# Column tiles for the global values, a contiguous DFT output, the FFN from slot 37 and its evictions later in the step

## The chip, the cores and the metric

The kernel runs on one NeuronCore of a Trainium2 chip. The metric is the device time of one execution in microseconds; lower is better. The five engines are TensorE (PE), VectorE (DVE), ScalarE (ACT), GpSimd (POOL) and SyncE (SP), each with its own in-order queue; here SP issues all DMAs.

## What is computed

Attention over 8 batches, 8 heads, 512 local and 32 global tokens of width 64, then a mixing layer on the concatenated heads:

```python
s_g   = scale * q_g @ k_all.T ;  out_g = softmax(s_g) @ v_all          # 32 global queries see all 544 keys
s_ll  = where(|i - j| <= 32, scale * q_l @ k_l.T, -1e9)                # local queries: a band ...
s_lg  = scale * q_l @ k_g.T ;    out_l = softmax([s_lg, s_ll]) @ [v_g, v_l]   # ... and the 32 global keys
x     = heads concatenated                                             # (8, 544, 512)
u     = x + real(fft(fft(x, axis=1), axis=2))
un    = (u - mean(u)) / sqrt(var(u) + 1e-6)
out   = u + relu(un @ w_ch1) @ w_ch2                                   # 512 -> 2048 -> 512
```

Matrix products are made of fp16 pieces: each operand is split into a high and a low half (hi, lo), and three products (hi hi, hi lo, lo hi) are added up in PSUM. So every operand has a copy on ScalarE for hi and a subtraction on VectorE or GpSimd for lo.

## The kernel before

**Order.** `run` (L831) writes down every step of the whole kernel with a time in *slots*, sorts by time, and issues the steps in that order; each engine's queue gets its own instructions in this order and nothing is reordered later. `add(slot, rank, f)` places a step at slot + rank, `at(time, f)` on the FFN's own scale. `warp` ties the two: up to slot F0 = 38 they are the same; from there 16 + PAUSE = 22 slots of attention pass beside 32 units (two chunks) of FFN; from slot 60 on, two units a slot. A slot has one attention tile `u` (128 queries of one pair of heads; 128 tiles, with a pause of 6 slots after the first 16).

**Weights.** 32 loads of 128x512 64-bit numbers (n = 0 to 15 are the first layer, k = 0; 16 to 31 the second, k = 1), one a slot from slot -8: `w_load` three slots ahead (SP), `w_abs` (ACT), `w_bits` (L184, four VectorE instructions that make fp32 of the bits), then column scales (`w_max`, `w_fold`, `w_scale`) and `w_split` (L251): for the second layer two ScalarE copies and a GpSimd subtraction. Second-layer weight t is handled at slot 8 + t and split f at slot 26 + f//2, with the scales at 23 to 25. Loads alternate between two buffers that lie where batch 0's DFT input comes later (`rw`) and two (`raw`) that share their place with the FFN's transposed input (`uh`).

**Attention.** For pair p (four slots): `scores` (L380) every second slot, with row halves of the array for the two heads; `masked` on VectorE; `exps`, `p_hi` on ScalarE; `p_lo` on GpSimd; `turn`, a DMA transpose; `values` (L428) at rank 0.60 five slots later; `norm` at 0.66 on VectorE. Global queries go once a pair: `g_scores`, `g_max`, `g_exp`, `g_hi`, `g_lo`, `g_turn`, then `g_values` (L487) and `g_norm` (L496). `g_values` multiplies the 64 rows of both heads' global queries with the values of both heads (130 columns), so half of each product belongs to the wrong head and is not used. `values` and `g_values` write one PSUM bank, `bk`; `values` waits for the `norm` and `g_norm` in front of it.

**DFT.** Once a batch (R = slot of its last tile): `d_load`, sums and differences on VectorE (`d_even`, `d_even2`, `d_tail`) and GpSimd (`d_odd`...), halves (`d_hi`, `d_lo`, `d_tail_hi`, `d_tail_lo`), then `d_first` (L659, five calls of eight matmuls with 137 columns), `d_z`, `d_z2`, `d_second`, `d_as`, `d_df`, `d_add`. `d_first` makes even and odd outputs in two passes and writes each to every second column of its PSUM tile; `d_z` and `d_z2` copy the tile out as it lies.

**FFN.** 17 chunks of 256 rows. Before each: `l_stats`, `l_un`, `l_hi`, `l_lo`, `l_turn` (a DMA transpose), `l_root`. A chunk has eight steps fp of two units: `f_first` (L786, 24 matmuls of 256 columns into one of two PSUM buffers `ps1`), `f_hi` (L799, ScalarE) and `f_lo` (L803, VectorE) that evict it as two halves `h`, and `f_second` (L807, 12 matmuls of 512 columns), which comes after the next step's `f_first`. In units of the step they stand at 0.30, 0.54, 0.65 and 3.30. From slot 60 on half of this is the rank within the slot: `f_hi` at 0.27, `f_lo` at 0.325.

Of the kernel before, what the change touches and what calls it, by code (L numbers as in the profile page):

```python
# [8 lines left out]
F32 = mybir.dt.float32  # L9
# [3 lines left out]
I32 = mybir.dt.int32  # L13
# [14 lines left out]
NVB = 2  # L28
NKB = 2
W0 = -8  # L30
F0 = 38
PAUSE = 6
RS0 = 1.829591166069289e-20


# [54 lines left out]
class Kern:  # L90
# [73 lines left out]
        return self.wd[1][i * P:(i + 1) * P, :]  # L164

    def w_load(self, k, i, n):
        if n % 4 < 2:
            if n == 0:
                rw = self.p1.tile([P, 2, 512, 2], I32, name="rw", tag="x4")
                self.rw = [rw[:, j] for j in range(2)]  # L170
            raw = self.rw[n % 2]
        else:
            raw = self.p2.tile([P, 512, 2], I32, name="raw", tag="uh")
        self.nc.sync.dma_start(raw.rearrange("p n t -> p (n t)"), self.w_src(k, i).bitcast(I32))
        self.raw[k, i] = raw
# [311 lines left out]
    def g_values(self, p):  # L487
        nc, s = self.nc, self.st[p]
        pl, vN = s.pop("plg"), s["v"][0]
        s["pvg"] = pv = self.bk[:64, 260:390].rearrange("p (h d) -> p h d", h=2)  # L490
        for c in range(5):
            n = P if c < 4 else 96
            for m, (a, w) in enumerate(((0, 0), (0, 1), (1, 0))):
                nc.tensor.matmul(pv, pl[:n, 5 * a + c], vN[:n, c, w], start=c == 0 and m == 0, stop=c == 4 and m == 2)  # L494

    def g_norm(self, p):  # L496
        nc, s = self.nc, self.st[p]
        b, hp, pv, sc = s["b"], s["hp"], s.pop("pvg"), s["v"][2]
        dn = self.p2.tile([64, 1], F32, name="dng")
        if hp == 0:  # L500
            self.g[b]["x"] = self.p1.tile([64, 4, 2, D], F32, name="xg")
        nc.vector.tensor_scalar(dn, pv[:, 0, 64:65], 1e-9, sc[:64], op0=ALU.add, op1=ALU.mult)
        nc.vector.reciprocal(dn, dn)
        nc.vector.tensor_scalar_mul(self.g[b]["x"][:, hp], pv[:, :, 0:64], dn)  # L504

    def g_own(self, b):
        xg = self.g[b]["x"]
        return [xg[h * SG:(h + 1) * SG, :, h] for h in range(2)]

    def g_out(self, b):  # L510
        for h, x in enumerate(self.g_own(b)):
            self.nc.sync.dma_start(self.xs[b][0:SG].rearrange("t (p h d) -> h t p d", h=2, d=D)[h], x)
# [146 lines left out]
    def d_first(self, b, i):  # L659
        nc, d = self.nc, self.D[b]  # L660
        eh, ht = d["eh"], d["ht"]
        cs, o, d0, m = (*divmod(i, 2), 0, P) if i < 4 else (0, 0, P, 1)
        d["ps"] = ps = self.d_psum(b)[:m, 0:NK]
        base = (0, 258, 514, 770)[2 * cs + o]
        w = 128 + (base == 0)
        n = NK // 2
        for kp in (1, 0):
            c0, po = n - n * kp, ps[:, 1 - kp:NK:2]
            for k, (a, c) in enumerate(((0, 0), (0, 1), (1, 0))):
                e = base + kp * w + d0  # L670
                nc.tensor.matmul(po, eh[:, a, e:e + m], self.c1[:, cs, c, c0:c0 + n], start=k == 0, stop=False)  # L671
            e = (0, 129, 257, 385)[2 * cs + o] + d0
            nc.tensor.matmul(po, ht[:, e:e + m], self.c1t[:, cs, c0:c0 + n], start=False, stop=True)
# [156 lines left out]

    def run(self):  # L831
        self.h = {}
        late = F0 + 16 + PAUSE

        def warp(t):
            if t < F0:
                return t
            return F0 + 32 * (t - F0) / (16 + PAUSE) if t < late else F0 + 32 + 2 * (t - late)

        plan = Plan(warp)  # L840
        add, at = plan.add, plan.at
# [109 lines left out]
        at(F0 + 32 * 7 + 4.5, self.l_load)  # L951
        for c in range(17):
            F = F0 + 16 * c
            L = F - (6 if c > 1 else 5)
            at(L + .42, self.l_stats, c)
            for j in range(2):
                at(L + j + 1.425, self.l_un, c, j)
                at(L + j + 1.76, self.l_hi, c, j)
                at(L + j + 1.79, self.l_lo, c, j)
                at(L + j + 2.03, self.l_turn, c, j)  # L960
# [62 lines left out]
```

## Time and profile before

| | |
|---|---|
| time, median of 3 (lowest, highest) | 1195.37 us (1194.23, 1196.3) |
| the profiled execution's own time | 1197.24 us |
| its span from first to last instruction | 1195.4 us |
| busy: PE, DVE, ACT, POOL | 84%, 64%, 51%, 42% |
| mean granted PE clock | 0.967 |
| the two costliest groups: `f_first` L796, `f_second` L815 | 383.2 and 381.6 us busy |

Busy time is an average over stages. The trace is cut into stages by the plan's slots; in each, the engine that is busy nearly all the time sets the pace, and where none is, a wait does. Matmuls are pipelined, so what one costs is read from the distance between starts and not from its duration. "[3.09 <-DVE xg L504]" in a timeline row says that the engine stood idle for 3.09 us in front of this instruction until VectorE had finished the one of line 504 that writes xg.

### The profile page before, as it was taken

Reading aid. Unit: us, or ns where it says so; the run is one execution under the profiler, and the core shown is the slowest. Engines: PE = TensorE matmul, PEld = TensorE weight load, DVE = VectorE, ACT = ScalarE, POOL = GpSimd, SP = SyncE. Lnnn points to the kernel's source line nnn. Section 1 sums busy time; section 2 is a strip of 40 time slices with the busy share of each in tenths; the row PEclk is TensorE's granted clock in tenths of the full one; section 3 lists DMA queues with packets and bytes.
Section 4 is the critical chain, followed back from the end, with each engine's and each line's share of the span. In section 5 each row is a group of like instructions: output and inputs, shape, how many; then the busy total and the mean of one; then the engine's idle time right before and its main releaser. Section 6 shows DMA issues by size and latency. Waiting matters only on the chain.

```text
span 1195.4 us, 24283 instructions
## 1 busy us (share of the span) xinstructions
PE 1001.7 (84%) x9351; PEld 717.5 (60%) x9351; DVE 763.1 (64%) x2089; ACT 609.1 (51%) x1348; POOL 508.0 (42%) x473
## 2 busy tenths in 40 slices
PE   0244325399798989998999899999999999999996
PEld 0134225276576767776777677767767666666664
DVE  6999974856757674867486748674766546433221
ACT  4767569576575655655566455646544112111110
POOL 2789278655544634463446344634462211100000
PEclk9999997599898999999999899999999999999999
DMA  7579934557555555555565546555455231120000
GB/s 263 154 178 244 268 75 104 127 116 176 115 138 111 144 117 122 116 139 119 120 115 139 119 119 111 144 119 121 80 110 110 60 87 36 38 55 19 27 27 18
DMA packets 249564, 137.55 MB, mean 115 GB/s; under 512 B 200576, under 2 KB 223200, under 8 KB 249448
## 3 DMA queue, kind: packets, MB, share of 16 engines
q1 hardware_dynamic: 249448, 136.01, 49.0%
q8 instruction: 73, 1.20, 0.4%
q14 instruction: 43, 0.35, 0.1%
HBM read 65.10 MB, written 18.35 MB: 70 GB/s over the span
## 4 chain that ended last, share of the span: by engine, by line
PE 60%; DVE 23%; ACT 8%; POOL 3%; DMA 3%; issue 2%; DVEq 0%; SPq 0%; POOLq 0%; ACTq 0%
PE acc L815 24%; PE ps L796 24%; PE S L394 2%; PE psd L671 2%; DVE pe L404 2%; PE psd L695 1%; PE bk L494 1%; ACT pe L413 1%; PE bk L439 1%; DVE ps L191 1%; DVE ps L192 1%; DVE ps L190 1%; DVE wm L193 1%; PE bk L441 1%; DVE h L805 1%
## 5 line engine op out<-in xcount | busy, mean ns | idle before, releaser
L796 PE MATMUL ps<-uh,wh 128*128 128x256 f16 x3264 | 383.2, 275 | 0.3 <-DMA uh<-unh 0.3
L815 PE MATMUL acc<-wh,h 128*128 128x512 f16 x1632 | 381.6, 384 | 0.0
L796 PEld LDWEIGHTS <-wh 128*128 128x128 f16 x3264 | 320.3, 99 | 59.9 <-issue 0.8
L805 DVE SCALAR_TENSOR_TENSOR h<-ps,h 128x512 f16<-128x512 f32 x136 | 93.7, 689 | 296.2 <-ACT h L801 296.1
L815 PEld LDWEIGHTS <-h 128*128 128x128 f16 x1632 | 155.0, 100 | 173.4 <-issue 11.1
L421 POOL TENSOR_TENSOR ph<-pe,ph 128x448 f16<-128x448 f32 x128 | 134.7, 1053 | 281.5 <-ACT ph L417 111.2
L801 ACT ACTIVATE h<-ps 128x512 f16<-128x512 f32 x136 | 80.3, 591 | 255.8 <-PE ps L796 255.7
L413 ACT ACTIVATE pe<-pe,nm 128x224 f32<-128x224 f32 x256 | 102.0, 469 | 82.3 <-DVE nm L404 82.3
L439 PE MATMUL bk<-vN,pl 128*128 128x65 f16 x768 | 74.5, 205 | 66.7 <-DVE xg L504 34.2
L404 DVE CUSTOM_DVE_ANT_0 pe<-S,msk,z 128x224 f32<-128x224 f32 x256 | 99.6, 445 | 2.9 <-PE S L394 2.9
L441 PEld LDWEIGHTS <-pl 96*128 96x128 f16 x768 | 61.6, 106 | 55.7 <-issue 54.4
L394 PE MATMUL S<-kT,qT 64*128 64x192 f16 x768 | 56.4, 273 | 28.6 <-ACT pg L475 28.3
L439 PEld LDWEIGHTS <-pl 128*128 128x128 f16 x768 | 64.4, 106 | 21.6 <-DMA pl<-ph 15.1
L394 PEld LDWEIGHTS <-qT 64*128 64x128 f16 x1536 | 54.7, 102 | 33.6 <-issue 29.4
L417 ACT ACTIVATE ph<-pe 128x448 f16<-128x448 f32 x128 | 72.0, 562 | 0.0
L372 POOL TENSOR_TENSOR kT<-qk,kT 128x512 f16<-128x512 f32 x32 | 42.7, 1333 | 51.0 <-ACT kT L367 49.8
L762 ACT ACTIVATE unh<-un 128x512 f16<-128x512 f32 x34 | 21.3, 625 | 70.4 <-DVE un L757 70.4
L441 PE MATMUL bk<-vB,pl 96*128 96x65 f16 x576 | 55.7, 205 | 0.0
L357 ACT ACTIVATE qk<-qk,z 128x512 f32<-128x512 f32 x64 | 45.5, 710 | 17.1 <-DVE z L322 17.1
L347 POOL TENSOR_TENSOR vN<-vf,vN 128x640 f16<-128x640 f32 x32 | 46.2, 1443 | 0.3 <-ACT vN L343 0.3
L588 POOL TENSOR_TENSOR s<-x 128x1020 f32<-128x1020 f32 x8 | 18.8, 2348 | 62.0 <-DMA x<-xs 56.3
L372 POOL TENSOR_TENSOR qT<-qk,qT 128x512 f16<-128x512 f32 x32 | 38.7, 1209 | 10.3 <-ACT qT L367 8.6
(182 smaller groups left out, 1638.6 us busy)
## 6 DMA issues: line engine op xcount, KB each, us to landing
qk<-in_qk SPq DMA_DIRECT2D x32, 512.0 KB
vf<-in_v SPq DMA_DIRECT2D x32, 320.0 KB
rw<-in_moe_w_ch SPq DMA_DIRECT2D x16, 512.0 KB
raw<-in_moe_w_ch SPq DMA_DIRECT2D x16, 512.0 KB
xs<-x SPq DMA_DIRECT2D x32, 256.0 KB
out<-u SPq DMA_DIRECT2D x16, 512.0 KB
x<-xs SPq DMA_DIRECT2D x24, 256.0 KB
u<-xs SPq DMA_DIRECT2D x24, 256.0 KB
```

Of the source, the lines that this page charges most:

```text
L372: self.nc.gpsimd.tensor_sub(lo, s.pop(nm), hi)
L394: nc.tensor.matmul(ps, qT[r, a, j], k, start=m == 0, stop=m == 2)
L404: nc.vector.tensor_tensor_reduce(self.per[(4 * p + j) % 4][:, h, 0:224], S[:, h, 224 * n:224 * n + 224], self.msk[:, j], z[:, 8:9], 3e38, ...
L413: nc.scalar.activation(pe[:, h, 0:224], pe[:, h, 0:224], AF.Exp, bias=nm[:, n, h:h + 1], scale=-1.0)
L417: self.nc.scalar.activation(ph[:, 0, :, 0:224], self.per[i % 4][:, :, 0:224], AF.Copy)
L421: self.nc.gpsimd.tensor_sub(ph[:, 1, :, 0:224], self.per[i % 4][:, :, 0:224], ph[:, 0, :, 0:224])
L439: nc.tensor.matmul(pv[:, j % 2, h], pl[:, 4 * a + 2 * h], vN[:, j, c, h, :], start=m == 0, stop=False)
L441: nc.tensor.matmul(pv[:, j % 2, h], pl[0:96, 4 * a + 2 * h + 1], vb, start=False, stop=m == 2)
L796: nc.tensor.matmul(ps[:, q], wt[:, w, c0:c0 + P], uh[:, :, 4 * a + kt, :], start=n == 0, stop=n == 11)
L801: self.nc.scalar.activation(h[:, 0], self.fps, AF.Relu)
L805: self.nc.vector.scalar_tensor_tensor(h[:, 1], self.fps, 0.0, h[:, 0], op0=ALU.max, op1=ALU.subtract)
L815: nc.tensor.matmul(self.acc_f[j], h[:, a, q, j * P:(j + 1) * P], self.w[1, f][:, w, :], start=f == 0 and a == 0 and w == 0, stop=f == 15 a ...
```

## The change

- F0 goes from 38 to 37 and a new LAG = 1 makes 23 slots of attention pass beside the first two chunks; slot 60 still begins chunk 2.
- Second-layer weight t is handled at slot 8 + 3t//2 (8 to 30) and split f at slot 33 + f (33 to 48); the scales move to slots 30 to 32. The last weights (n > 23) use two of the `uh` buffers and one of the buffers `u`, none of `rw`.
- Normalisation before chunk 0 has its own places (`l_un` at 33.5 and 33.6, the transposes at 33.8 and 34.1), and that before chunk 1 comes one unit earlier against its chunk (6 units ahead rather than 5). To allow two halves under way, `hl` is kept by j.
- `g_values` multiplies each head's 32 global queries with that head's values alone: 30 matmuls of 65 columns in place of 15 of 130, one head to PSUM partitions 0 to 31 and the other to 32 to 63. `g_norm`, `g_out` and `g_square` follow: 64 columns a pair, one square in place of two.
- `d_first` writes its even and odd outputs to two contiguous halves of the PSUM tile; `d_z` and `d_z2` read the halves and write every second fp16 element, so that z is the same as before.
- `f_hi` and `f_lo` stand at 0.97 and 1.20 of a step (0.485 and 0.60 of a slot from slot 60 on).

```diff
-F0 = 38
+F0 = 37
+LAG = 1
...
     def w_load(self, k, i, n):
-        if n % 4 < 2:
+        if n > 23 and n % 3 == 2:
+            raw = self.p2.tile([P, 512, 2], I32, name="rx", tag="u", bufs=3)
+        elif n < 24 and n % 4 < 2:
...
-        s["pvg"] = pv = self.bk[:64, 260:390].rearrange("p (h d) -> p h d", h=2)
+        s["pvg"] = pv = self.bk[:64, 260:325]
...
-                nc.tensor.matmul(pv, pl[:n, 5 * a + c], vN[:n, c, w], start=c == 0 and m == 0, stop=c == 4 and m == 2)
+                for h in range(2):
+                    r = slice(h * SG, h * SG + SG)
+                    nc.tensor.matmul(pv[r], pl[:n, 5 * a + c, r], vN[:n, c, w, h], start=c == 0 and m == 0, stop=c == 4 and m == 2)
...
-        nc.vector.tensor_scalar_mul(self.g[b]["x"][:, hp], pv[:, :, 0:64], dn)
+        nc.vector.tensor_scalar_mul(self.g[b]["x"][:, hp], pv[:, 0:64], dn)
...
-            c0, po = n - n * kp, ps[:, 1 - kp:NK:2]
+            c0 = n - n * kp
+            po = ps[:, c0:c0 + n]
...
-        self.nc.scalar.activation(d["hl"][0], d["ps"], AF.Copy, scale=0.125)
+        self.nc.scalar.activation(self.woven(d["hl"][0]), self.halves(d["ps"]), AF.Copy, scale=0.125)
+
+    def woven(self, t):
+        return t.rearrange("p (k o) -> p o k", o=2)
+
+    def halves(self, t):
+        return t.rearrange("p (o k) -> p o k", o=2)
...
-        late = F0 + 16 + PAUSE
+        late = F0 + 16 + PAUSE + LAG
...
-            return F0 + 32 * (t - F0) / (16 + PAUSE) if t < late else F0 + 32 + 2 * (t - late)
+            return F0 + 32 * (t - F0) / (16 + PAUSE + LAG) if t < late else F0 + 32 + 2 * (t - late)
...
-            s = W0 + n
+            s = W0 + (n if k == 0 else 16 + 3 * t // 2)
...
-            add(s + 3 + f // 2, .75, self.w_split, 1, f)
+            add(s + 3 + f, .75, self.w_split, 1, f)
...
-            L = F - (6 if c > 1 else 5)
+            if c == 0:
+                L, x, y, z = F - 4, (.50, .60), (.02, .06), (.30, .50)
+            else:
+                L, x, y, z = F - 6, (1.425, 2.425), (.335, .365), (.605, .605)
...
-                at(t + .54, self.f_hi, c, fp)
-                at(t + .65, self.f_lo, c, fp)
+                at(t + .97, self.f_hi, c, fp)
+                at(t + 1.20, self.f_lo, c, fp)
```

More of the change, by code (lines that the diff above doesn't have):

```diff
@@ L500, in g_norm, with g_out @@
         if hp == 0:
-            self.g[b]["x"] = self.p1.tile([64, 4, 2, D], F32, name="xg")
-        nc.vector.tensor_scalar(dn, pv[:, 0, 64:65], 1e-9, sc[:64], op0=ALU.add, op1=ALU.mult)
+            self.g[b]["x"] = self.p1.tile([64, 4, D], F32, name="xg")
+        nc.vector.tensor_scalar(dn, pv[:, 64:65], 1e-9, sc[:64], op0=ALU.add, op1=ALU.mult)
         nc.vector.reciprocal(dn, dn)
-        nc.vector.tensor_scalar_mul(self.g[b]["x"][:, hp], pv[:, :, 0:64], dn)
-    def g_own(self, b):
+        nc.vector.tensor_scalar_mul(self.g[b]["x"][:, hp], pv[:, 0:64], dn)
+    def g_out(self, b):
         xg = self.g[b]["x"]
[L508 to L512, printed above, removed]
+        for h in range(2):
+            self.nc.sync.dma_start(self.xs[b][0:SG].rearrange("t (p h d) -> h t p d", h=2, d=D)[h], xg[h * SG:(h + 1) * SG])
     def g_square(self, b):
-        for h, x in enumerate(self.g_own(b)):
-            r = slice(h * SG, (h + 1) * SG)
-            self.nc.scalar.activation(self.junk[r, 0:256].rearrange("p (a d) -> p a d", a=4), x, AF.Square, accum_out=self.accx[b % 2][r, 4:5])
+        x = self.g[b]["x"].rearrange("p a d -> p (a d)")
+        self.nc.scalar.activation(self.junk[:64, 0:256], x, AF.Square, accum_out=self.accx[b % 2][:64, 4:5])
     def x_square(self, p):
@@ L684, in d_z2 @@
         hi, lo = d.pop("hl")
-        self.nc.vector.scalar_tensor_tensor(lo, d.pop("ps"), 0.125, hi, op0=ALU.mult, op1=ALU.subtract)
+        self.nc.vector.scalar_tensor_tensor(self.woven(lo), self.halves(d.pop("ps")), 0.125, self.woven(hi), op0=ALU.mult, op1=ALU.subtract)
     def d_second(self, b, kt, cs):
@@ L760, in l_hi @@
         L = self.L[c]
-        L["hl"] = hl = self.p2.tile([P, 2, DM], F16, name="unh")
+        L["hl", j] = hl = self.p2.tile([P, 2, DM], F16, name="unh")
         self.nc.scalar.activation(hl[:, 0], L["un"], AF.Copy)
@@ L765, in l_lo @@
         L = self.L[c]
-        self.nc.vector.tensor_sub(L["hl"][:, 1], L.pop("un"), L["hl"][:, 0])
+        self.nc.vector.tensor_sub(L["hl", j][:, 1], L.pop("un"), L["hl", j][:, 0])
     def l_turn(self, c, j):
@@ L771, in l_turn @@
             L["uh"] = self.p2.tile([P, 2, 8, P], F16, name="uh", tag="uh")
-        self.nc.sync.dma_start_transpose(L["uh"][:, j], L.pop("hl").rearrange("p a d -> p (a d)"))
+        self.nc.sync.dma_start_transpose(L["uh"][:, j], L.pop(("hl", j)).rearrange("p a d -> p (a d)"))
     def l_root(self, c):
@@ L858, in run @@
                     add(s + 3 + kt, .75, self.w_split, 0, 4 * kt + c)
-        s = W0 + 31
         add(s, .41, self.w_max, 1, 0)
@@ L953, in run @@
             F = F0 + 16 * c
-            L = F - (6 if c > 1 else 5)
+            if c == 0:
+                L, x, y, z = F - 4, (.50, .60), (.02, .06), (.30, .50)
+            else:
+                L, x, y, z = F - 6, (1.425, 2.425), (.335, .365), (.605, .605)
             at(L + .42, self.l_stats, c)
             for j in range(2):
[L957 to L960, printed above, removed]
+                at(L + x[j], self.l_un, c, j)
+                at(L + x[j] + y[0], self.l_hi, c, j)
+                at(L + x[j] + y[1], self.l_lo, c, j)
+                at(L + x[j] + z[j], self.l_turn, c, j)
             at(L + 3.43, self.l_root, c)
```

## The prediction

> **What bounds the kernel now.** I read the page, then the windows cut at the plan's stages, then the waits of PE from chunk 2 on, then the timeline at one of those waits.
>
> ```profile
> PE 60%; DVE 23%; ACT 8%; POOL 3%; DMA 3%; issue 2%; DVEq 0%; SPq 0%; POOLq 0%; ACTq 0%
> ...
> 38.00:166.00 128.00, 47.79 (x548) 38.42 (x549) 119.53 (x319) 85.88 (x192) 89.19 (x81) 1.00 0.75 195
> 166.00:206.00 40.00, 18.74 (x229) 15.74 (x230) 18.43 (x63) 39.29 (x78) 29.56 (x29) 0.89 0.48 112
> 206.00:241.00 35.00, 16.02 (x196) 13.51 (x192) 30.88 (x78) 22.02 (x48) 24.04 (x23) 0.55 0.56 118
> 241.00:301.00 60.00, 56.44 (x608) 40.92 (x606) 38.69 (x120) 43.04 (x104) 35.09 (x31) 0.97 0.66 146
> 301.00:382.00 81.00, 70.23 (x685) 51.09 (x686) 56.90 (x162) 45.72 (x108) 36.28 (x37) 0.92 0.52 110
> 382.00:901.00 519.00, 504.92 (x4955) 360.84 (x4954) 354.08 (x1004) 295.76 (x672) 250.97 (x225) 0.98 0.56 122
> ```
> ```profile
> 0.00:165.90 165.90, 13.21 (x240) 12.11 (x240) 1.00 0.74 205
> 0.00:205.80 205.80, 16.62 (x312) 15.33 (x313) 0.98 0.69 187
> ```
> ```profile
> 241.11 1.25 PE L796 MATMUL ps<-uh,wh 128*128 128x256 f16 x5
> ...
> 301.31 0.39 PE L796 MATMUL ps<-uh,wh 128*128 128x256 f16 x2 [0.33 <-DMA uh<-unh]
> ...
> 382.42 0.61 PE L796 MATMUL ps<-uh,wh 128*128 128x256 f16 x4
> ```
>
> Columns of the windows: length, then busy time (and count) of PE, weight loads, DVE, ACT, POOL, then PE clock. The short pair counts score matmuls (L394, 24 a group): ten groups are done at 165.90 and thirteen at 205.80, and the plan puts the eleventh at slot 26 and the fourteenth at slot 32. The last fence has the starts of FFN chunks 0, 1 and 2 (plan: slots 38.3, 49.3, 60.15).
>
> The chain that ended last lies on PE for 60% and on VectorE for 23%, and the windows say where each. There are three regimes. Up to slot 26 VectorE is the bound (119.53 of 128). From 26 to 32 it is ScalarE (39.29 of 40) while VectorE has 21.6 us free. From 241 PE is the bound, apart from stalls (70.23 of 81 in chunk 1).
>
> **Part 1: weights spread out, FFN one slot earlier.** Second-layer weight t comes at slot 8+3t//2 in place of 8+t, and its split at 33+f in place of 26+f//2.
>
> ```profile
> L190 DVE TENSOR_SCALAR_CACHE_REDUCE ps<-ps 128x512 f32<-128x512 f32 x32 | 22.0, 689 | 4.1 <-ACT ps L182 4.1
> L191 DVE TENSOR_SCALAR ps<-ps 128x512 int32<-128x512 int32 x32 | 22.4, 700 | 1.1
> L192 DVE SCALAR_TENSOR_TENSOR ps<-rw,ps 128x512 int32<-128x512 int32 x16 | 11.1, 696 | 0.6
> L193 DVE SCALAR_TENSOR_TENSOR wm<-raw,ps 128x512 int32<-128x512 int32 x16 | 11.0, 686 | 0.5
> ...
> L248 ACT ACTIVATE wh<-wm,wsc 128x512 f16<-128x512 f32 x32 | 22.7, 708 | 0.0
> L257 ACT ACTIVATE wm<-wm,wsc 128x512 f32<-128x512 f32 x16 | 11.5, 722 | 0.5
> ...
> L258 POOL TENSOR_TENSOR wh<-wm,wh 128x512 f16<-128x512 f32 x32 | 36.8, 1154 | 10.7 <-ACT wm L257 9.4
> ```
>
> A weight costs VectorE 0.689+0.700+0.696+0.686 = 2.77 us. Five of the sixteen (t = 11 to 15, slots 24, 26, 27, 29, 30) leave the VectorE-bound stretch: 13.9 us, of which I count 13, some slots now being too light to fill. Between slots 26 and 32, twelve splits of 0.708+0.722 = 1.43 us (17.2 us) leave ScalarE, so 22 are left there; four weights (11.1) join VectorE's 18.43, giving 29.5. At the 93% at which VectorE ran before that is 32 us in place of 40: 8, of which I count 7, since the DFT chain of batch 0 also waits in there. From slot 32 to the FFN VectorE has 30.88 of 35; with the start one slot earlier, 33. Removed before the FFN: 13+7+2 = 22; I take 20, and 10 to 28 as bounds (10 if POOL, 89.19 of 128, takes VectorE's place). The FFN follows PE's queue and not its input here: 241.11 shows no wait, and chunk 0's normalisation now ends two slots before slot 37.3, later only by what VectorE lags.
>
> What it costs: chunk 0 now runs over 11.5 slots rather than 11 and carries about 11.5 of the splits, 16.5 us of ScalarE. To the 43.04 of its 60 us come these and 2 for the half slot, together 61; PE was busy for 56.44 and gets about 1 more for the half slot. Two engines with some 60 us each, in queues that wait for one another, do not fit into 60: I take 66 for 60.2, **+6** (bounds 0 and +12). POOL takes 11.5 x 1.154 = 13.3 more beside 35.09 of 60, which fits. On SP's queue the loads of the ninth and tenth second-layer weights now reach a buffer 0.32 slot before it is free (slots 17 and 18); queued behind them are transposes due 0.6 slot later, which cover that at no cost, and without this cover it would be a third of a slot, 2 us, each. In chunk 1 the half slot costs 1 and the earlier normalisation removes the 0.33 wait and some VectorE load; with its DFT (part 2) I take **-1**.
>
> **Part 2: contiguous DFT output.**
>
> ```profile
> 441.34 0.32 PE L673 MATMUL psd<-c1tr,ht 96*128 96x137 f16 x1
> 441.46 0.55 PE L671 MATMUL psd<-c1r,eh 128*128 128x137 f16 x3
> 441.81 0.32 PE L673 MATMUL psd<-c1tr,ht 96*128 96x137 f16 x1
> ...
> 998.27 2.62 PE ps L796 x24
> 1000.89 2.59 PE acc L815 x12
> ```
>
> Four matmuls of 137 strided columns pass in 441.81-441.34 = 0.47 us, 117 ns each. FFN matmuls of 256 contiguous columns take 2.62/24 = 109 ns, 0.426 ns a column: 137 columns would be 58. Eight a call, with one already shorter: 7.5 x 59 = 0.44 us; five calls a batch, 2.2 us; six batches after 382: **-13.2** (batch 1 is in chunk 1's term, batch 0 is hidden before the FFN). The copies L680 and L685 now write strided fp16 with the same element count, off PE's path, and g_square runs once a batch where it ran twice; I price both at nothing, as ScalarE has 295.76 of 519 busy and VectorE 354.08.
>
> **Part 3: global values in two column tiles.** Fifteen matmuls of 130 columns become thirty of 65, alternating between PSUM partitions 0 to 31 and 32 to 63.
>
> ```profile
> 411.86 0.42 PE L394 MATMUL S<-kT,qT 64*128 64x192 f16 x6
> 412.12 0.23 PE L394 MATMUL S<-kg,qT 64*128 64x32 f16 x6
> ...
> 418.36 1.05 PE L494 MATMUL bk<-vN,plg 128*64 128x130 f16 x15
> 419.34 0.39 PE L240 MATMUL bk<-vac,part 128*128 128x6 f32 x2
> ```
>
> Now 0.98 us a call. Column tiles are not in this trace; row halves are: six matmuls of 192 columns pass in 0.26 us, where 0.426 x 192 x 6 would be 0.49. If columns overlap like that, 15 x 65 x 0.426 = 0.42 us plus loads; if not, double that, 0.83 plus loads, as now. So -0.5 to 0 a call; I take -0.35, nearer the row halves. Of 20 calls after 382 five fall where VectorE is the bound: 15 x 0.35 = **-5**. The Trainium skill ("TensorEngine Tiling (Array Packing)", Instruction Overhead) speaks against it: about 60 cycles per matmul, so a dimension near that is not to be divided. By that page's 2.4 GHz clock thirty would be 0.75 us, an estimate, and the term -3.5.
>
> **Part 4: evictions later.** f_hi goes from 0.27 to 0.485 of a slot (from slot 60 on), past ScalarE's prep_mul and halo; f_lo from 0.325 to 0.60, past d_even, d_lo and d_tail_lo, ahead of norm and masked.
>
> ```profile
> PE bk L439 <- DVE xg L504: 13.6, 5, 3.1
> ```
> ```profile
> 412.52 0.69 DVE L805 SCALAR_TENSOR_TENSOR h<-ps,h 128x512 f16<-128x512 f32 x1 [2.05 <-ACT h L801]
> 413.13 0.55 DVE L599 TENSOR_TENSOR x<-x 128x257 f32<-128x257 f32 x1
> ...
> 427.65 0.34 DVE L504 TENSOR_SCALAR xg<-bk,dng 64x128 f32<-64x128 f32 x1
> ...
> 886.72 0.69 DVE L805 SCALAR_TENSOR_TENSOR h<-ps,h 128x512 f16<-128x512 f32 x1 [2.17 <-ACT h L801]
> ```
> ```profile
> 428.04 0.19 PE L439 MATMUL bk<-vN,pl 128*128 128x65 f16 x1 [3.09 <-DVE xg L504]
> ...
> 900.78 0.19 PE L439 MATMUL bk<-vN,pl 128*128 128x65 f16 x1 [1.59 <-DVE xg L504]
> ```
> ```profile
> 901.00:905.00 4.00, 4.00 (x51) 2.47 (x48) 2.98 (x6) 2.71 (x5) 1.05 (x1) 1.00 0.37 53
> 549.00:552.00 3.00, 3.00 (x9) 1.06 (x7) 2.28 (x4) 1.89 (x4) 1.04 (x1) 0.50 0.47 87
> 665.00:671.50 6.50, 5.74 (x45) 3.13 (x45) 4.90 (x13) 3.32 (x6) 1.04 (x1) 0.50 0.22 41
> 785.00:787.50 2.50, 2.50 (x37) 1.83 (x35) 1.48 (x4) 2.29 (x5) 0.50 (x1) 0.50 0.03 7
> 429.50:432.50 3.00, 3.00 (x8) 1.06 (x7) 2.24 (x5) 2.30 (x5) 1.04 (x1) 0.50 0.47 87
> ```
>
> Once a batch PE stands still for VectorE, five times, 13.6 us. VectorE works without a gap from 412.52 to 427.65; just ahead it sat idle 2.05 us in f_lo's wait, with d_even2 (L599) ready behind it. With f_lo behind d_even2 that idle time goes, and each stall is 2.05 to 2.17 shorter (the last one goes): 4 x 2.05 + 1.6 = **-9.8**. What is late next is the rest of the same VectorE work, 0.5 to 1 us a batch. Bounds are 0, if the new order only moves the idle time elsewhere, and -13.6; a loss I exclude, because VectorE's work ahead of each stall is the same in sum. No PE work waits for the later f_lo itself: its second layer comes a slot later, and norm behind f_lo already gates the values ahead of it.
>
> After each of the four long stalls PE's clock reads 0.50 for 3.0, 6.5, 2.5 and 3.0 us; after the 1.59 us one it reads 1.00. 15 us at half speed lose **-7.5**, which goes if 1 us stalls act like the 1.59 one. The skill ("TensorE: Matmul & The Clock Gate", Why this matters for your kernels) wants no gap above about 3 us; by that rule the four stalls trip the gate and the remaining ones don't, and the trace agrees: 13.6 less 1.59 leaves 12.0 for the four, 3.0 each.
>
> **Sum.** -20 +6 -1 -13.2 -5 -9.8 -7.5 = -50.5. The profiled execution took 1197.24 us (span 1195.4), 1.87 over the median 1195.37, so 1146.7 and, at the median, **1145 us**.
>
> **Rivals.**
> - *ScalarE takes the gain back.* The splits fill ScalarE in chunk 0, f_hi now queues behind them, and PE's second layer waits for h. Against: splits f and second layer keep 0.7 slot or more. With chunk 0 at 75 (+15) and only 10 won before it: -50.5 +10 +9 = -31.5, 1164 us. Chance 0.12.
> - *The 117 ns is not the stride* (weight loads, say). FFN loads of the same 128 columns keep up with 109 ns only, so this trace cannot exclude it wholly; but 137 columns at two 0.426 ns steps are 117 exactly. -13.2 and 2 go: 1160 us. Chance 0.05.
> - *Slower: column tiles drain the array at every alternation.* A change of matmul form costs here: 15 x 58 ns (0.426 x 130 + 3) is 0.87, and the next form starts 0.11 later. Thirty such in a call add 3.3 us, and in the 25 calls after the FFN's start 82: -50.5 +5 +82 = +36.5, 1232 us. It decides from 45.5/(25 x 30) = 0.06 us an alternation. The skill's tiling page (Key Properties) says a change of mode drains, but not a change of tile. Against: the row halves at L394 alternate too, with no such loss. Chance 0.05.
> - *No change:* nothing is won before the FFN, chunk 0 costs its 12, tiles and stalls stay as they are: +12 -1 -13.2 = -2.2, 1193 us, within the 0.2% (2.4 us) that is about what a measurement of this kernel can tell from nothing. Chance 0.03.
>
> **How the numbers follow.** The forecast has 0.75. Its bounds: best -28 +0 -4 -15 -9 -13.6 -8 = -77; worst -10 +12 +2 -12 0 -5 -4 = -17. These are not all reached together, so 1120 to 1174, which takes in the first two rivals. Faster by over 0.2%: 0.75+0.12+0.05 = 0.92, less 0.01 for slower ends: 0.91; same 0.03; slower 0.06.
>
> **What would show it.** FFN's first matmul near 221; ScalarE over 95% busy in chunk 0; L671 and L673 58 to 62 ns apart; L494's thirty in about 0.6 us; no 2 us wait of L805 ahead of d_even2, stalls on L504 near 1 us, and PE clock 1.00 from chunk 2 on. A first FFN matmul after 231, a chunk 0 above 72, or L494 calls over 1 us would make the prediction wrong.

## The result, and the profile after

| | before | after |
|---|---|---|
| median (lowest, highest), 4 runs each | 1195.84 us (1194.23, 1198.6) | 1159.34 us (1152.76, 1160.44) |
| the profiled execution, its span | 1197.24, 1195.4 us | 1160.44, 1158.6 us |

The ratio of after to before is 0.9681, with a 95% interval of 0.964 to 0.9722. So the kernel is faster, by 36.5 us where 50.5 were forecast, and the time lies inside the range. Lines in the kernel after stand 1 to 8 higher than before: scores L397, `values` L442 and L444, `g_exp` L478, `g_values` L499, `g_norm` L509, `d_first` L673 and L675, first layer L804, `f_hi` L809, `f_lo` L813.

The chain that ended last, from the page of after:

```profile
PE 51%; DVE 28%; ACT 6%; DMA 6%; POOL 4%; issue 4%; SPq 1%; DVEq 0%; POOLq 0%
```

The windows of after, cut at the same places of the plan as before: from 37 us to slot 26, to slot 32, to the FFN's first matmul, chunk 0, chunk 1, chunks 2 to 10 (columns: length, PE, weight loads, DVE, ACT, POOL, PE clock).

```profile
37.00:158.00 121.00, 43.90 (x603) 34.60 (x603) 105.23 (x287) 83.53 (x187) 88.11 (x80) 1.00 0.83 202
158.00:194.00 36.00, 18.23 (x249) 15.02 (x251) 30.61 (x90) 25.87 (x57) 19.47 (x19) 0.91 0.56 139
194.00:220.70 26.70, 12.88 (x185) 10.12 (x180) 22.39 (x75) 18.67 (x41) 17.09 (x17) 0.51 0.59 134
220.70:293.20 72.50, 60.38 (x680) 43.69 (x678) 47.41 (x137) 60.61 (x131) 49.97 (x45) 0.90 0.63 131
293.20:370.90 77.70, 68.75 (x741) 48.02 (x735) 55.04 (x153) 48.04 (x110) 42.32 (x42) 0.89 0.53 109
370.90:880.50 509.60, 496.70 (x5335) 352.29 (x5334) 361.89 (x1033) 298.81 (x674) 252.80 (x226) 0.99 0.61 127
```

The same stages by the exact starts of the chunks, with the forecast beside them:

| stage | before | after | difference | forecast |
|---|---|---|---|---|
| up to the FFN's first matmul | 241.1 | 220.7 | -20.4 | -20 |
| chunk 0 | 60.2 | 72.5 | **+12.3** | +6 |
| chunk 1 | 81.1 | 77.7 | -3.4 | -1 |
| chunks 2 to 10 | 530.6 | 509.6 | -21.0 | } -35.5 |
| the rest | 282.5 | 278.1 | -4.4 | } |

So 16 us are missing in two places, 6 in chunk 0 and 10 behind chunk 2, and 2.8 more than forecast were won before the FFN and in chunk 1. A stage's length comes from one profiled execution, and the executions of one kernel lie 1 to 13 us apart, so a difference of 2 or 3 us in one stage shows nothing by itself. What PE waits for from chunk 2 on (total, times, longest): in the kernel before there was beside the 13.6 us on `g_norm`, shown above, one wait of 0.3 us on `g_exp` and one of 0.2 on `norm`. The fence has all that is in after:

```profile
PE S L397 <- ACT pg L478: 6.8, 3, 3.5
PE bk L442 <- DVE xg L509: 4.4, 2, 2.4
PE S L464 <- DVE nm L407: 1.5, 4, 0.4
```

The old stall is down from 13.6 to 4.4 us, but a new one has come: the score matmuls wait three times, 6.8 us, for the exponentials of the global queries. Of the four long stalls three are still followed by half clock. PE's rows at the first and the last of the four, then windows behind the first and the last (the clock stands behind POOL's count):

```profile
403.53 0.66 PE L397 MATMUL S<-kT,qT 64*128 64x192 f16 x6 [3.54 <-ACT pg L478]
...
758.99 0.19 PE L442 MATMUL bk<-vN,pl 128*128 128x65 f16 x1 [1.97 <-DVE xg L509]
```
```profile
403.00:406.00 3.00, 2.47 (x27) 1.63 (x27) 2.08 (x7) 2.97 (x9) 1.77 (x2) 0.50 0.02 5
...
759.00:762.00 3.00, 3.00 (x45) 1.97 (x45) 1.63 (x3) 2.57 (x5) 0.79 (x1) 1.00 0.03 6
```

The two edits of matmul form did on PE what they were to do. PE's timeline shows a DFT call and a call of the global values:

```profile
428.31 0.22 PE L675 MATMUL psd<-c1tr,ht 96*128 96x137 f16 x1
428.38 0.34 PE L673 MATMUL psd<-c1r,eh 128*128 128x137 f16 x3
428.56 0.22 PE L675 MATMUL psd<-c1tr,ht 96*128 96x137 f16 x1
```
```profile
246.67 0.64 PE L499 MATMUL bk<-vN,plg 128*32 128x65 f16 x30
247.24 0.39 PE L243 MATMUL bk<-vac,part 128*128 128x6 f32 x2
```

Four DFT matmuls pass in 428.56-428.31 = 0.25 us, 62 ns each where it was 117; thirty column-tiled matmuls take 247.24-246.67 = 0.57 us where fifteen took 0.98.

### The profile page after: what moved, and what is told of

It reads as the page before. It is cut to its first block, busy times and chain, and to the rows that moved or that the text cites. A ratio compares the mean times of both kernels' runs of the same rounds, so it can differ in the third digit from the quotient of the medians.

```text
span 1158.6 us, 25225 instructions
## 1 busy us (share of the span) xinstructions
PE 971.7 (84%) x9831; PEld 688.1 (59%) x9831; DVE 756.4 (65%) x2089; ACT 606.2 (52%) x1332; POOL 508.3 (44%) x473
## 4 chain that ended last, share of the span: by engine, by line
PE 51%; DVE 28%; ACT 6%; DMA 6%; POOL 4%; issue 4%; SPq 1%; DVEq 0%; POOLq 0%
PE acc L823 21%; PE ps L804 21%; DVE pe L407 3%; DMA xt<-xs 2%; PE S L397 2%; DVE h L813 2%; PE psd L703 2%; DMA qk<-in_qk 1%; ACT pe L416 1%; PE psd L673 1%; DVE ps L194 1%; PE S L464 1%; DVE ps L193 1%; DVE ps L195 1%; DVE wm L196 1%
## 5 line engine op out<-in xcount | busy, mean ns | idle before, releaser
L804 PE MATMUL ps<-uh,wh 128*128 128x256 f16 x3264 | 385.6, 276 | 0.0
L804 PEld LDWEIGHTS <-wh 128*128 128x128 f16 x3264 | 320.5, 99 | 60.3 <-issue 0.4
L424 POOL TENSOR_TENSOR ph<-pe,ph 128x448 f16<-128x448 f32 x128 | 135.2, 1056 | 249.9 <-ACT ph L420 94.4
L813 DVE SCALAR_TENSOR_TENSOR h<-ps,h 128x512 f16<-128x512 f32 x136 | 93.1, 685 | 165.8 <-ACT h L809 165.4
L809 ACT ACTIVATE h<-ps 128x512 f16<-128x512 f32 x136 | 80.1, 589 | 215.0 <-PE ps L804 214.9
L442 PE MATMUL bk<-vN,pl 128*128 128x65 f16 x768 | 73.9, 204 | 60.2 <-DVE xg L509 33.9
L397 PE MATMUL S<-kT,qT 64*128 64x192 f16 x768 | 58.0, 278 | 37.4 <-ACT pg L478 36.8
L444 PEld LDWEIGHTS <-pl 96*128 96x128 f16 x768 | 61.0, 105 | 47.0 <-issue 36.3
L397 PEld LDWEIGHTS <-qT 64*128 64x128 f16 x1536 | 55.9, 103 | 43.4 <-issue 38.4
L442 PEld LDWEIGHTS <-pl 128*128 128x128 f16 x768 | 63.6, 105 | 22.9 <-DMA pl<-ph 17.3
L719 DVE SCALAR_TENSOR_TENSOR asm<-psd,dsc,asm 128x258 f32<-128x258 f32 (+1 forms) x21 | 10.1, 482 | 75.1 <-PE psd L703 60.5
L375 POOL TENSOR_TENSOR kT<-qk,kT 128x512 f16<-128x512 f32 x32 | 40.1, 1254 | 39.2 <-ACT kT L370 34.6
L444 PE MATMUL bk<-vB,pl 96*128 96x65 f16 x576 | 55.2, 204 | 0.0
L360 ACT ACTIVATE qk<-qk,z 128x512 f32<-128x512 f32 x64 | 45.2, 708 | 10.7 <-DVE z L325 10.7
L261 POOL TENSOR_TENSOR wh<-wm,wh 128x512 f16<-128x512 f32 x32 | 37.0, 1156 | 26.6 <-ACT wm L260 25.3
```

The source lines that it names most:

```text
L397: nc.tensor.matmul(ps, qT[r, a, j], k, start=m == 0, stop=m == 2)
L424: self.nc.gpsimd.tensor_sub(ph[:, 1, :, 0:224], self.per[i % 4][:, :, 0:224], ph[:, 0, :, 0:224])
L442: nc.tensor.matmul(pv[:, j % 2, h], pl[:, 4 * a + 2 * h], vN[:, j, c, h, :], start=m == 0, stop=False)
L444: nc.tensor.matmul(pv[:, j % 2, h], pl[0:96, 4 * a + 2 * h + 1], vb, start=False, stop=m == 2)
L804: nc.tensor.matmul(ps[:, q], wt[:, w, c0:c0 + P], uh[:, :, 4 * a + kt, :], start=n == 0, stop=n == 11)
L809: self.nc.scalar.activation(h[:, 0], self.fps, AF.Relu)
```

## The experiments

Every kernel below computes the whole reference. "Behind chunk 2" means from the first matmul of chunk 2 to the end. Each ratio is to the kernel before, run on the same chip. A letter in an expectation stands for a theory; A is the view that the evictions' move only swaps one stall for another.

### One part alone, or all but one

The question of the first four: which part brings less than its term. `evict_only` and `evict_back` have the one edit of part 4, on the kernel before and taken back on the kernel after:

```diff
-                at(t + .54, self.f_hi, c, fp)
-                at(t + .65, self.f_lo, c, fp)
+                at(t + .97, self.f_hi, c, fp)
+                at(t + 1.20, self.f_lo, c, fp)
```

> The kernel before with only the two evictions moved to 0.97 and 1.20. Theory A: 0 to -4 us against before (1191 to 1196), with a stall in the score matmuls in place of the one on g_norm. Rival B: -17 us, 1179. Rival C: +5 us or more, above 1200.

> The changed kernel with the two evictions put back to 0.54 and 0.65 of a step, all else changed. Theory (A, from the trace after): moving them took away one VectorE stall a batch and put another of the same size in its place (PE now waits in the score matmuls for ScalarE's g_exp, which waits for VectorE's g_max behind the moved f_lo), so the time is that of the changed kernel, 1159 us, within 5 us, and the stall on line 509 (xg) is back at about 3 us a batch while that on g_exp is gone. Rival (B, the prediction's): the move won about 17 us, so 1172 to 1178 us. Rival (C): the move costs more than it wins, so 1145 to 1152 us.

`dft_only` is the kernel before with part 2; `start_back` is the kernel before with parts 2, 3 and 4 and so has all but the early start; `tiles_only` has part 3 alone.

```diff
-            c0, po = n - n * kp, ps[:, 1 - kp:NK:2]
+            c0 = n - n * kp
+            po = ps[:, c0:c0 + n]
```

> The kernel before with only the DFT's first stage writing contiguous columns. Both theories: the 137-column matmuls stand 59 to 62 ns apart in place of 117, 2.2 us a batch in seven batches, 13 to 15 us less than before, about 1181 us. Rival: VectorE bounds the slots after the DFT as well, and PE's saving is given back in longer waits: 5 us or less.

> The changed kernel without the part on weights and start: F0 at 38, second-layer weights one a slot and splits two a slot, normalisation of chunks 0 and 1 as before; the DFT, the tiles and the moved evictions stay. If the start is worth what the traces show at the first matmul of chunk 2 (382.4 to 370.9, less about 4 us of it from DFT and tiles before that point), it takes 7 to 12 us more than the changed kernel, 1166 to 1171. By the prediction's terms (20 won, 6 lost in chunk 0): 14 more, 1173. Rival: the start is worth nothing, 1159.

```diff
-                nc.tensor.matmul(pv, pl[:n, 5 * a + c], vN[:n, c, w], ...)
+                for h in range(2):
+                    r = slice(h * SG, h * SG + SG)
+                    nc.tensor.matmul(pv[r], pl[:n, 5 * a + c, r], vN[:n, c, w, h], ...)
```

> The kernel before with only the global values in two column tiles (with the norm, output and square that go with them). In the changed kernel's trace a call takes about 0.45 us of PE in place of 0.98, so 25 calls after the FFN's start hold 13 us. Theory D: much of it is given back, because between the score matmuls of slot 62 (and every 16 slots on) and the values of slot 66 VectorE sets the pace and PE only waits longer: the parts measured so far (1.2% DFT, 1.1% evictions alone, 0.6% start) leave about 4 us, so 1186 to 1192. Rival: the whole 13 us, 1183 or less. Rival: nothing, 1196.

| kernel | median us | ratio (95%) | chunk 0 | chunk 1 | chunks 2 to 10 | rest |
|---|---|---|---|---|---|---|
| `evict_only` | 1183.5 | 0.9894 (0.9861 to 0.9928) | 58.1 | 80.9 | 520.6 | 282.5 |
| `dft_only` | 1181.33 | 0.9876 (0.9837 to 0.9914) | 59.3 | 78.4 | 521.3 | 278.9 |
| `tiles_only` | 1194.17 | 0.9973 (0.9956 to 0.999) | 60.4 | 80.3 | 530.4 | 281.7 |
| `evict_back` | 1170.18 | 0.9776 (0.9734 to 0.9818) | 68.6 | 77.3 | 515.9 | 278.1 |
| `start_back` | 1166.01 | 0.9744 (0.9702 to 0.9786) | 58.8 | 78.9 | 509.7 | 278.1 |

The DFT is worth its term: (521.3-530.6)+(278.9-282.5) = -12.9 behind chunk 2 where -13.2 was forecast. The evictions alone bring 520.6-530.6 = -10.0 there and not -17.3; theory A, by which they bring nothing, fell. It fell in `evict_back` too: the stalls on `g_norm` are back there (13.2 us), but the ones on `g_exp`, which it put down to the moved `f_lo`, did not go (4.9 us for 6.8). By medians the evictions are worth 1170.18-1159.34 = 10.8 us on top of the rest, below theory B's 13 to 19. The tiles alone bring almost nothing, less than the 4 to 10 us expected, although each call is 0.4 us shorter. The early start brings the difference of `start_back` and after, 0.9744 to 0.9681, some 7 us by medians, with intervals that overlap; by the start of chunk 2 it is 379.2-370.9 = 8.3.

Why the evictions bring less. First the waits of PE behind chunk 2 in `evict_only`, then its VectorE from `g_max` (L469) to `g_norm` (L504), where the idle time was to go:

```profile
PE bk L439 <- DVE xg L504: 7.6, 4, 2.1
```
```profile
408.65 0.27 DVE L469 TENSOR_SCALAR ng<-ng,z 64x1 f32<-64x1 f32 x1
408.84 1.20 DVE L599 TENSOR_TENSOR x<-x 128x257 f32<-128x257 f32 x1
...
419.80 1.79 DVE L631 SCALAR_TENSOR_TENSOR eh<-x,dsc,eh 128x514 f16<-128x514 f32 x1
...
424.77 0.34 DVE L504 TENSOR_SCALAR xg<-bk,dng 64x128 f32<-64x128 f32 x1
```

The rows of the kernel before from the same `g_max` on, again of VectorE:

```profile
410.20 0.27 DVE L469 TENSOR_SCALAR ng<-ng,z 64x1 f32<-64x1 f32 x1
...
423.89 1.19 DVE L631 SCALAR_TENSOR_TENSOR eh<-x,dsc,eh 128x514 f16<-128x514 f32 x1
```

The 2.05 us of idle time did go: `d_even2` (L599) follows `g_max` at once. But from the start of L469 to that of `g_norm` (L504) it is 424.77-408.65 = 16.1 us where it was 427.65-410.20 = 17.5: 1.3 less and not 2.05, because the same work now meets other GpSimd work and takes longer (L631 1.79 for 1.19, the four sums L599 to L604 0.2 more). From `masked` in slot 62 to `g_norm` VectorE's stretch is 26.6 us for 27.4, in the next batches 26.5, 26.5 and 25.5 for 28.0, 27.5 and 26.9. The stalls fell by about as much, to 2.08, 2.10, 2.09 and 1.30, and the last went.

The tiles show the other half of it: the waits of PE behind chunk 2 in `tiles_only`.

```profile
PE bk L439 <- DVE xg L506: 13.6, 5, 3.4
PE S L394 <- ACT pg L475: 6.3, 4, 2.1
```

PE saves 0.4 us a call, but in these slots it is VectorE's stretch that sets the pace; PE is there sooner and waits longer, 19.9 us for 13.9.

### Chunk 0: is it ScalarE?

By the prediction ScalarE and PE share the blame. `split_pool` moves the scaled copy of the second-layer split from ScalarE to GpSimd:

```diff
-        if k == 0:
-            nc.gpsimd.tensor_mul(f, f, s.to_broadcast([P, 512]))
-        else:
-            nc.scalar.activation(f, f, AF.Copy, scale=s)
+        nc.gpsimd.tensor_mul(f, f, s.to_broadcast([P, 512]))
```

> The changed kernel with the second-layer split's scaled copy (line 260, 0.72 us each) on GpSimd, as the first layer has it, in place of ScalarE. If ScalarE (60.6 of the 72.5 us of chunk 0 busy) is what makes chunk 0 long, that chunk takes 66 to 68 us and the kernel 4 to 7 us less, 1152 to 1155. Rival: GpSimd (50.0 of 72.5) or VectorE's waits take over, chunk 0 stays within 2 us of 72.5 and the kernel at 1159.

The median is 1160.39 us, ratio 0.9688 (0.9664 to 0.9712). The window of its chunk 0:

```profile
220.20:294.60 74.40, 61.49 (x683) 43.55 (x678) 52.66 (x142) 51.69 (x118) 63.19 (x56) 0.86 0.57 128
```

ScalarE is busy for 51.69 and no longer 60.61 us, and the chunk is not shorter (74.4 for 72.5). That does not acquit ScalarE, because the same edit gives GpSimd 13.2 us more to do: in chunk 0 PE's waits for `g_exp` on ScalarE fell from 5.6 to 0.5 us, and those for VectorE grew from 6.5 to 12.4. So the answer has to be read from after itself. PE stands still there four times for over 1 us: 1.73 (the scores wait for `g_exp`), 3.40 (the values, for `g_norm`), 1.42 (the values, for `norm`) and 3.84 (the scores, for `g_exp`), 10.4 us in all. In chunk 0 of the kernel before it does so twice, 1.04 and 1.96, both for `g_exp`. In the first of the four ScalarE itself is late: `g_max` had ended at 236.50, and `g_exp` (L477) follows the copy of a split (L260) without a gap:

```profile
238.52 0.72 ACT L260 ACTIVATE wm<-wm,wsc 128x512 f32<-128x512 f32 x1
239.15 0.76 ACT L477 ACTIVATE pg<-S,ng,z 64x512 f32<-64x512 f32 x1
```

In front of the last one ScalarE stands idle for 0.83 us until `g_max` is done, so there VectorE is late. At the second, of 3.40 us, it is VectorE with GpSimd beside it:

```profile
248.18 1.21 DVE L317 TENSOR_SCALAR z<-z 128x4 int32<-128x4 int32 x1
249.43 0.16 DVE L327 SCALAR_TENSOR_TENSOR z<-z 128x2 f32<-128x2 f32 x1
...
249.76 1.01 DVE L329 TENSOR_SCALAR z<-z 128x4 f32<-128x4 f32 x1
```
```profile
248.09 1.27 POOL L484 TENSOR_TENSOR pgr<-pg,pgr 64x576 f16<-64x576 f32 x1
249.59 1.15 POOL L261 TENSOR_TENSOR wh<-wm,wh 128x512 f16<-128x512 f32 x1 [0.23 <-ACT wm L260]
```
```profile
247.49 2.75 PE L823 MATMUL acc<-wh,h 128*128 128x512 f16 x12
253.64 0.21 PE L442 MATMUL bk<-vN,pl 128*128 128x65 f16 x1 [3.40 <-DVE xg L509]
```
```profile
252.80:259.60 6.80, 5.96 (x55) 4.80 (x55) 3.95 (x18) 4.52 (x10) 2.97 (x5) 0.50 0.46 99
```

In the kernel before, the operation that is L317 here (L314 there) took 0.17 us all eight times from chunk 2 to chunk 10. Here four such operations of a few elements (L317 and L329 to L331) take 1.01 to 1.21 us, and each ends 0.03 to 0.04 us after the GpSimd operation beside it: L317 at 249.39 and L484 at 249.36, L329 at 250.77 and L261 at 250.74, L330 at 251.99 and L339 at 251.95, L331 at 252.97 and L424 at 252.94. In the gap of GpSimd's queue from 249.36 to 249.59, L327 takes 0.16. So each stood until GpSimd was through; call that a collision. The Trainium skill ("SBUF — State Buffer", Who interferes with whom) says it as a rule: the two engines share a port pair, and where a VectorE operation needs it too (in a two-port mode, or with two inputs in SBUF), the one that comes second is blocked outright until the first is done. The trace agrees in when the operations end, and in that three of the four start after GpSimd's (the record of L331 starts 0.01 us ahead of L424's); it does not show in which mode they ran.

The collisions are not new, however. In chunk 0 of the kernel before the same chain of operations meets three of over 1 us and one of 0.80:

```profile
261.29 1.24 DVE L314 TENSOR_SCALAR z<-z 128x4 int32<-128x4 int32 x1
262.56 1.15 DVE L324 SCALAR_TENSOR_TENSOR z<-z 128x2 f32<-128x2 f32 x1
```
```profile
260.07 2.75 PE L815 MATMUL acc<-wh,h 128*128 128x512 f16 x12
262.65 2.78 PE L796 MATMUL ps<-uh,wh 128*128 128x256 f16 x24
265.97 0.19 PE L439 MATMUL bk<-vN,pl 128*128 128x65 f16 x1 [0.53 <-DVE xg L504]
```

The chain, from the first operation on z to the end of `g_norm`, takes 5.7 us there (260.25 to 265.91) and 5.9 in after (247.67 to 253.58); without collisions, behind chunk 2, it takes 2.1 (425.87 to 427.99). What differs is PE's own work meanwhile. In the kernel before, an `f_second` and an `f_first`, 5.4 us together, stand in PE's queue ahead of the values that wait, and 0.53 us are left to wait; in after only the `f_second` stands there. PE's order is the plan's, in which the splits have no PE step: the new start and the 23 slots (F0 and LAG) put the `f_first` elsewhere. In `start_back`, without that part, both stand there, the wait is 0.53 us and chunk 0 takes 58.8 us. Once the work is gone, the collisions set the length of the stall: 1.68 us with two of them in `evict_back`, 3.40 with four in after, 4.62 with five in `split_pool`.

How much of the 12.3 us the moved splits cost by themselves, on ScalarE or on GpSimd, no run separates. The evictions' move may have a part in it: without it chunk 0 is 68.6 us long (`evict_back`), still 8 over the kernel before. But it is 70.0 us in `stats_early` below, whose edit does not touch chunk 0, so 2 or 3 us of this are scatter.

### Behind chunk 2: VectorE's stretch

If VectorE's stretch sets the pace, what shortens it should be worth more than what relieves PE. In after its timeline ahead of the 3.54 us stall shows what lies in it:

```profile
391.71 2.19 DVE L639 TENSOR_TENSOR st<-xt 32x255 f32<-32x255 f32 x1 [1.47 <-DMA xt<-xs]
...
396.16 1.43 DVE L642 TENSOR_TENSOR et<-xt 32x128 f32<-32x128 f32 x1
397.52 0.27 DVE L643 TENSOR_TENSOR et<-st 32x128 f32<-32x128 f32 x1
...
400.73 0.68 DVE L813 SCALAR_TENSOR_TENSOR h<-ps,h 128x512 f16<-128x512 f32 x1
...
402.14 0.26 DVE L472 TENSOR_SCALAR ng<-ng,z 64x1 f32<-64x1 f32 x1
```
```profile
402.44 0.77 ACT L477 ACTIVATE pg<-S,ng,z 64x512 f32<-64x512 f32 x1 [6.25 <-DVE ng L472]
```

VectorE waits 1.47 us for `xt`, then `d_tail`'s small sums run at GpSimd's pace (L642 takes 1.43 us and ends 0.14 after GpSimd's operation beside it, L643 of the same shape takes 0.27), `f_lo` stands ahead of `g_max`, ScalarE waits 6.25 us for `g_max`, and PE's scores wait for ScalarE. Three edits of after, and two joined:

```diff
# xt_first: in d_load, the three loads of xt ahead of the others
+        nc.sync.dma_start(d["xt"][0:15], xs[129:144, :])
+        nc.sync.dma_start(d["xt"][15:30], xs[401:416, :])
+        nc.sync.dma_start(d["xt"][30:32], xs[0:T:272, :])
...
# stats_early: every second chunk's statistics three slots earlier, out of the stretch
-            at(L + .42, self.l_stats, c)
+            at(L + .42 - (6 if c % 2 and c > 1 else 0), self.l_stats, c)
...
# flo_140: f_lo behind g_max
-                at(t + 1.20, self.f_lo, c, fp)
+                at(t + 1.40, self.f_lo, c, fp)
```

> The changed kernel with the three small DFT loads (xt) issued ahead of the four large ones. In the changed kernel VectorE waits 1.5 us for xt at the head of its densest stretch. Theory F: that wait goes and with it 1 to 1.5 us of each of the stalls behind it (3.5, 2.9, 2.4, 2.0 us), some of the half-clock time too: 5 to 9 us less, 1150 to 1154. Rival: the stretch is set by VectorE's sums running slower beside GpSimd's, and the wait comes back as slower sums: 2 us or less.

> The changed kernel with f_lo at 1.40 of a step (0.70 of a slot), behind norm, masked and g_max in VectorE's queue instead of ahead of them. Theory E: the stall of up to 3.5 us in the score matmuls comes from g_max standing behind f_lo and the DFT sums, so it gets 0.6 to 0.7 us shorter and the time 1 to 4 us less, 1155 to 1158. Rival: the DFT sums alone set it, or f_lo delays the next slot's sums by as much: 1159 within 2.

> The changed kernel with the normalisation statistics of the odd chunks from 3 on (2.2 us of VectorE, up to 4.0 beside GpSimd) six units, three slots, earlier: into VectorE's idle time ahead of the dense stretch (slots 62.7 to 65.7 and every 16 on) and out of it. Theory D (VectorE's work in that stretch sets the stalls): the two stalls of 2.0 to 2.4 us on line 509 go, the ones on g_exp ahead of the statistics stay; 4 to 7 us less, 1152 to 1155. Rival (something else in PE's way, such as the transfers or the score matmuls, decides): 1159 within 2.

> The same with the small DFT loads first. Theory D: with the wait for xt gone the stalls of 2.4 us on line 509, five in all, lose the 4.0 us of statistics and go; 8 to 12 us less than the small loads first alone (1157), 1145 to 1149. Rival: 1155 or more.

> The same with f_lo at 1.40. If what f_lo at 1.40 won (3 us) lies in chunks 0 and 1 as well, 1143 to 1147; if it lay in the stall on g_exp alone, as the one before.

| kernel | median us | ratio (95%) | chunk 0 | chunks 2 to 10 |
|---|---|---|---|---|
| after | 1159.34 | 0.9681 (0.964 to 0.9722) | 72.5 | 509.6 |
| `xt_first` | 1156.98 | 0.9663 (0.9642 to 0.9684) | 70.3 | 507.8 |
| `flo_140` | 1155.94 | 0.9646 (0.9625 to 0.9668) | 70.5 | 507.3 |
| `stats_early` | 1151.48 | 0.9654 (0.9589 to 0.9719) | 70.0 | 505.6 |
| `xt_stats` | 1147.2 | 0.9594 (0.9559 to 0.9629) | 70.3 | 498.0 |
| `xt_stats_140` | 1146.92 | 0.9588 (0.9561 to 0.9615) | 72.0 | 497.8 |

Each of the three alone has a median inside the interval of after, so none is clear of noise alone; `xt_first` was to bring 5 to 9 us and brought 2. The waits of PE behind chunk 2 say why, in `xt_first`, in `stats_early` and in `xt_stats`:

```profile
PE bk L442 <- DVE xg L509: 10.7, 5, 2.4
...
PE S L397 <- ACT pg L478: 0.9, 3, 0.4
```
```profile
PE S L397 <- ACT pg L478: 7.7, 4, 2.9
...
PE bk L442 <- DVE xg L509: 0.7, 2, 0.5
```
```profile
PE bk L442 <- DVE xg L509: 2.2, 4, 0.7
PE S L464 <- DVE nm L407: 1.5, 4, 0.4
PE S L397 <- ACT pg L478: 1.0, 3, 0.4
```

There are two due times in one stretch, `g_max` in its middle and `g_norm` at its end. `xt_first` frees the first (6.8 to 0.9), and the time is waited for at the second (4.4 to 10.7). Its rival is right in part, too: from `g_max` to `g_norm` VectorE now takes 16.1 us at the first batch where it took 13.9, because more of its operations meet GpSimd's (the four sums L600 to L605 4.2 us for 1.7). `stats_early` frees the second and leaves the first (7.7). Only both together take the stalls away: the 12.7 us of after become 4.7, VectorE's stretch from `masked` to `g_norm` is 24.7 us for 27.7 at the first batch, and the window of chunks 2 to 10 reads

```profile
368.30:866.30 498.00, 492.70 (x5334) 350.33 (x5333) 363.05 (x1035) 299.07 (x674) 255.46 (x226) 1.00 0.60 130
```

PE is busy for 492.70 of 498.00 us at full clock. This version beats both kernels: its interval (to 0.9629) ends below that of after (from 0.964). `f_lo` behind `g_max` adds nothing to it (0.9588 for 0.9594).

Last, `best_no_tiles` is `xt_stats_140` with `g_values`, `g_norm` and what follows them as before the change. Where PE sets the pace, the tiles should count.

> The kernel of the run before with the global values as in the kernel before: 15 matmuls of 130 columns a call. Theory D (the tiles' 13 us were given back in VectorE's stretch): with the stretch relieved they show, and this kernel takes 8 to 12 us more than the one with tiles. Rival (the tiles save PE nothing that counts): 4 us or less more, as the tiles alone gave.

The median is 1152.32 us, ratio 0.9638 (0.9609 to 0.9667), and chunks 2 to 10 take 503.3 us for 497.8. So the tiles are worth 5.4 us by medians and 5.5 by the stage. The intervals overlap by a hair (0.9615 and 0.9609), but the four executions of each don't (1145.56 to 1147.64, 1151.24 to 1154.82). That is between the two expectations, and it is the size of the forecast's -5, which the tiles alone didn't bring.

## Why the prediction was right, and where it was wrong

**Before the FFN: right in sum, not in its parts.** The FFN starts at 220.7 where 221 was forecast. But the stretch up to slot 26 gave 8 us and not 13 (158 for 166), the next 4 and not 7 (36 for 40), and the last 8.3 and not 2 (26.7 for 35.0). That they add up to the forecast is luck. In the first, four weights left and not five (the one at slot 24 stays: L193 runs for 20 weights there, where L190 ran for 24), and VectorE stands waiting for 11.6 us where it waited for 3.6. In the second VectorE has the load that was forecast (30.61 us for 29.5), but it is busy for 85% of the 36 us and not for 93%. In the last, one slot of the 6.3 is 5.6 us long, so that 2 us for a start one slot earlier was too little.

**Chunk 0: the direction was right, the cause was another one in the main, and the size was double.** ScalarE's load was forecast to the microsecond (61; it is 60.61), but by PE's waits it explains the first of four stalls alone (1.73 us, 1.04 before). The step that failed is "Two engines with some 60 us each, in queues that wait for one another, do not fit into 60: I take 66". It asks how much work each engine has and prices the half slot at 1 us of PE, and not which of PE's work stands in front of which wait. The new start took the `f_first` from in front of the values, and VectorE's chain, as long as before, became a stall of 3.40 us for 0.53. PE idles for 72.50-60.38 = 12.1 us of the chunk where it was 60.00-56.44 = 3.6, and the mean clock in the chunk is 0.90 where it was 0.97, for which the sum has no term there. "POOL takes 11.5 x 1.154 = 13.3 more beside 35.09 of 60, which fits" is right for GpSimd's own time (49.97 of 72.5); that its operations hold up VectorE's small ones does not stand in it. The stage came out at +12.3, just past the upper bound of +12 and past the 72 us that the text had named as a sign of error.

**DFT: right**, in mechanism (62 ns for 58) and sum (-12.9 for -13.2). The rival that it is not the stride is out.

**Tiles: the price of a call was right (-0.41 for -0.35), the term wasn't.** -5 became -1 in the kernel before (behind chunk 2), because in the slots where VectorE sets the pace PE's saving turns into waiting, and it does so in more places than the five calls in twenty that were left out: as a new stall of 6.3 us on `g_exp`. The drain rival is out, 30 alternations in 0.57 us, and the estimate of 0.75 us by 60 cycles a matmul was too long. (The page of the Trainium skill that the prediction names for it gives the 60 cycles and not the clock of 2.4 GHz.)

**Evictions: the term that failed.** -17.3 was forecast, -10.0 measured alone; on top of the other parts it is 509.6-515.9 = -6.3 by the stage of one execution each. Alone, the stalls fell from 13.6 to 7.6, which is -6.0 for -9.8, and the half clock from 17.1 to 6.8 us, worth at most half of the difference, -5.1 for -7.5. The step was "What is late next is the rest of the same VectorE work, 0.5 to 1 us a batch". What was late next was 1.3 to 2.1 us a batch in `evict_only` and 2.0 to 3.5 in after. The idle 2.05 us went as said, but work beside GpSimd grew by some of it; the wait for `xt` grew (3.6 us in four waits up to chunk 10, 0.4 in one before); PE, relieved by the two other parts, arrived sooner; and with `g_max` there is a second due time ahead of the one that the forecast looked at. The half clock, counted from the clock records of the trace, went with the stalls only in part: 17.1 us in chunks 2 to 16 before, 6.8 in `evict_only`, 10.2 in after, none in `xt_stats`. The line at about 3 us, by which the prediction told harmful stalls from harmless ones, was too high: stalls of 2.08 and 2.10 us were followed by half clock.

The rival with ScalarE (1164 us, chunk 0 at 75) came near the measured times by luck: its step, that PE's second layer waits for h, is not among PE's waits in chunk 0.

## What to carry to other kernels

Find the stretch of in-order work on another engine that paces the main one, and count all its due times: relieving one moves the wait to the next, so two edits that took 1.8 and 4.0 us off chunks 2 to 10 alone took off 11.6 together, and a saving on the main engine is worth little until the stretch is short enough. Before moving steps of the main engine, ask what its work covers: a chain of small VectorE operations beside GpSimd was almost three times its normal length before and after the change, and cost 0.5 us while two FFN steps stood in front of its consumer and 3.4 when one did. Busy shares show neither.

## What the hardware showed

- VectorE operations on 128x2 or 128x4 numbers took 1.0 to 1.2 us in place of 0.16 to 0.22 beside GpSimd's tensor operations: they ended 0.03 to 0.04 us after these.
- Column tiles overlap: 30 matmuls of 65 columns on two halves of the output partitions took 0.57 us, 19 ns each, less than 65 columns at 0.426 ns (28 ns). Writing every second fp32 column of PSUM cost two column times (117 ns for 137 columns), contiguous output one (62).
- The length of a stall alone did not decide the half clock. Stalls of 2.44, 2.89 and 3.54 us were followed by some 3.4 us at 0.50, one of 1.97 was not; in `evict_only` two of 2.08 and 2.10 were, and a third of 2.09 was not. Where the stall lies decides with it: the clock changes in these traces only on a grid of 3.413 us. Cut on that grid, from 300 to 1100 us of all fourteen kernels, every window at full clock in which PE was busy for less than 0.44 of it was followed by one at 0.50, none in which it was busy for more than 0.49 was, and between the two it went either way. The windows with most of the 2.08 and the 2.09 us stall in `evict_only` (length, PE busy, clock) have PE busy for 0.48 and 0.55:

```profile
423.39:426.80 3.41, 1.64 (x38) 1.00 0.00 0
...
658.90:662.32 3.42, 1.88 (x40) 1.00 0.00 0
```
